# RetNet attention and a SwiGLU feed-forward block on one core: one explicit list for the order of all steps, in place of a list that ends early in the second up stage

## The chip, the cores and the metric

The kernel runs on one core of a Trainium2 chip. The metric is the device time of one execution in microseconds (us), median of several runs; lower is better. All other times here are from the hardware profile of one execution.

## What is computed

```python
def _attn_ref(q, k, v):                      # (4, 8, 768, 64) each
    for t in range(S):
        state = gamma * state + einsum('bhd,bhe->bhde', k[:, :, t], v[:, :, t])
        y[:, :, t] = scale * einsum('bhd,bhde->bhe', q[:, :, t], state)
    ...
x = attn_out.transpose(0, 2, 1, 3).reshape(3072, 512)
g = x @ w_gate                               # 512 x 1536
out = ((g * sigmoid(g)) * (x @ w_val)) @ w_out     # 1536 x 512
```

The three weights are float64 in the input; the rest is float32.

## The kernel before

**Stages.** The 3,072 tokens are worked off in four segments of 768 tokens, numbered 0 to 3: three chunks of 128 positions of two batches each. Each segment has an *up* stage (gate and value products, SiLU, their product, over 12 blocks `f` of 128 hidden columns) and a *down* stage (the product with `w_out`, over the same 12 blocks, into six banks of PSUM, one for each 128 tokens). The attention of segment `s + 1` is computed inside the down stage of segment `s`. The attention of segment 0 and the conversion of the weights from float64 words stand at the start, beside the up stage of segment 0.

**Products.** Every large product is made as three matmuls of fp32r parts: each operand is split into three tiles, by a step on ScalarE (ACT), then one on VectorE (DVE), then one on GpSimd (POOL) or DVE. From segment 1 on an up block is seven products in the manner of Strassen. Each is six matmuls of 384 columns.

**Steps and their names.** The program is a set of named steps, and each step issues some instructions, mostly on one engine:

- `s/pF.N` (line 933): product N of up block F of segment s, on TensorE (PE). Products 0, 2, 4 and 6 add into one bank, 1 is alone in a bank, and 3 and 5 add into a third.
- `s/uF.N` (lines 954 to 961): the ten steps between these products. `u.0`, `u.3` and `u.4` are copies by ACT out of a bank (shown at lines 955, 956 and 957). `u.0` must be through before product 2 of its block, `u.3` before product 4, `u.4` before product 5; `u.5`, on DVE, before product 6. `u.2` and `u.8` are SiLUs on ACT.
- `s/wF.G.0`, `.1`, `.2` (lines 921 to 931): the split of weight group G of up block F, on ACT (line 846), DVE (line 849) and POOL (line 852). Group 0 is for products 0 to 2, group 1 for 3 to 5, group 2 for 6. `s/LF` (line 911) loads the block's weights.
- `s/DF.T` (line 1000): three matmuls of 512 columns, block F, 128 tokens number T, into bank T. `s/hF.0` to `.2` split the hidden tile of block F, `s/WF` (line 980) loads the split `w_out` rows of block F into a ring of three tiles. In segment 0 these rows are split there as well (`0/dF.0` to `.2`) and stored for later (`0/ZF`).
- `s/eT` (line 1007): the copy of bank T into slot `T % 4` of the tile `chunk_x`, and the store of 128 finished rows. Even T are copied by ACT (line 1023) and odd T by DVE (line 1021). T = 5 of the last segment is done in halves: one by ACT, which issues its own store (lines 1015 and 1016), and one by DVE with a store from SyncE's queue (SP; lines 1017 and 1018).
- Attention of the next segment, for pair of chunks P: `scP.G` scores, `decP.G.I` the decay mask, `mP` and `oP` mixing with the values and the old state, `tP` the new state, all fp32 matmuls at line 638 or the steps that follow them; `yP.K` copies the result out of PSUM on ACT (line 874), `sumP.M` and `xP.N.K` make the operand of the next up stage. `s/lN` loads the N-th of its inputs. Keys without a slash are the same kind of steps for the start and the weight conversion (`s0`, `m0`, `A0`, `A1`, `l1:0`, `G7:1`).

**What sets the order.** Engines work in the order in which instructions were issued to them, and so does SP, which issues nearly all DMAs and waits in that order. Waits between engines are added by the framework from the tiles that each step reads and writes. `down_stage`, `up` and `up3` enter each step with a due time that is worked out from tables (`at(t, key, ...)`). `run` then issues:

```python
for key in PLAN.split():
    if key in events:
        events.pop(key)[2]()
    else:
        do(key)
for key in sorted(events, key=lambda k: events[k][:2]):
    events[key][2]()
```

So the steps that `PLAN` names come first, in its order, and all others follow by their due times. `PLAN` names 825 of the 2,312 steps: the start, up and down stage of segment 0, and of the up stage of segment 1 the products up to `1/p3.4`. Its last words are `1/p3.4 0/e4`.

Of the kernel before, what the change touches and what calls it, by code (L numbers as in the profile page):

```python
# [46 lines left out]


PLAN = """
    l0:0 A1 A0 s0 l1:0 l0:2 U0:0 A2 s1 l0:3 l2:0 K0 a0:1 l2:1 m0 b0:1 S0:1 c0:1 x0:1 V0:0 l1:3  # L50
    k1 a0:0 x0:2 C0:1 b0:0 n0:0 l1:2 t0 l2:2 l3:1 s2 l2:3 l3:0 Q2 m1 U1:1 g2 S0:0 c0:0 l3:2 n0:1
    k2 t1 o2 l4:0 x1:1 x1:2 g3 m2 C0:0 s3 n0:3 l4:1 q3 t2 o3 a1:1 n0:2 p0:0 x2:2 n0:4 b1:1 S1:1
    l3:3 g4 a1:0 c1:1 x2:1 n0:5 m3 k3 s4 C1:1 v0:0 b1:0 x3:1 x3:2 u0:0 l5:0 l5:1 U2:0 S1:0 t3
    c1:0 n1:0 s5 n1:1 l5:2 g5 C1:0 y0:0 p0:1 T0:0 a2 n1:3 T0:1 n1:4 q4 v0:1 q5 u0:1 U12:3 l4:2
    n1:2 o5 n1:5 T1:0 m5 y0:1 p1:0 b2 u1:0 U3:1 a12 S2 o4 p1:1 m4 a3 x5:1 v1:0 T0:2 T1:1 v1:1
    u1:1 U4:0 x4:1 c2 x5:2 x4:2 p0:2 b12 C2 y1:1 p1:2 T1:2 b3 n2:0 v1:2 y1:0 u0:2 Z0 U5:1 S3
    v0:2 n2:1 c12 n2:2 G2:0 u1:2 c3 L3 n2:3 S12 y0:2 U13:2 C3 a4 y1:2 b4 G2:1 C12 Z1 n3:0 n2:4
    S4 T2:0 T2:1 n2:5 i2:1 n3:3 n3:1 Z12 T2:2 U6:0 i2:0 c13 U14:3 a13 W2:0 W2:1 j2:1 n3:4 n3:2
    Z2 j2:0 G3:1 b13 a5 c4 G3:0 S13 T3:0 C4 i3:0 n4:0 T3:1 n4:1 n4:3 T3:2 b5 U7:1 S5 a6 i3:1 c14
    n3:5 n4:4 W3:0 W3:1 j3:0 C13 j3:1 n4:2 T4:0 G4:0 c5 C5 n4:5 T4:1 G4:1 W4:1 i4:0 Z3 i4:1 Z13  # L60
    U8:0 T4:2 j4:1 W4:0 a7 n5:0 n5:1 b6 n5:3 S6 j4:0 a14 b14 n5:2 G5:0 n5:4 S14 Z4 n5:5 c6 i5:0
    a8 C14 T5:0 C6 G5:1 n6:0 b7 n6:1 i5:1 n6:2 n6:3 U9:1 T5:1 U15:2 Z14 W5:0 W5:1 S7 c7 G6:0
    n6:4 T5:2 U10:0 i6:0 Z5 a15 j5:0 C7 T6:0 G6:1 b8 n7:0 n6:5 n7:3 W6:0 i6:1 j5:1 T6:1 b15 T6:2
    l5:3 n7:1 l4:3 S8 Z6 c8 n7:4 n7:2 n7:5 T7:0 C8 a9 W6:1 k4 c15 j6:0 S15 T7:1 U11:1 b9 k5
    U16:3 j6:1 G7:1 C15 G7:0 n8:0 W7:0 i7:1 S9 i7:0 n8:3 t4 Z15 U17:2 n8:1 W7:1 j7:0 c9 C9 n8:2
    a10 n8:4 b10 t5 G8:0 j7:1 G8:1 n9:0 T7:2 i8:1 Z7 n9:3 n8:5 S10 c10 W8:0 T8:0 a16 n9:1 i8:0
    n9:4 b16 C10 n9:2 a11 n9:5 W8:1 j8:0 j8:1 P0 G9:1 S16 G9:0 T8:1 T9:0 n10:0 b11 T8:2 n10:3
    n10:1 L2 W9:1 i9:0 T9:1 i9:1 0/h0.0 S11 c16 T9:2 W9:0 n10:2 0/h0.1 G10:1 C16 Z8 c11 C11
    G10:0 n10:4 n10:5 n11:0 j9:1 Z16 W10:1 n11:3 P2 j9:0 0/h0.2 n11:4 P1 T11:0 i10:0 c17 n11:1
    T11:1 0/h1.0 L1 T11:2 n11:2 W10:0 i10:1 G11:1 j10:0 n11:5 G11:0 L0 0/W0 a17 T10:0 0/h1.1 b17  # L70
    Z11 0/W1 T10:1 0/d0.0 h0 S17 W11:0 T10:2 0/d0.1 j10:1 1/sc0.0 h1 i11:0 Z9 0/d1.0 i11:1 j11:0
    C17 0/d0.2 1/l3 W11:1 1/dec0.0.0 1/old0 0/d1.1 1/sc0.1 1/dec0.0.1 0/D0.0 0/h2.0 Z17 1/q0.1
    0/W2 j11:1 0/Z0 0/D0.1 0/D0.2 0/h3.0 1/dec0.1.1 1/dec0.1.0 1/k0.1 1/q0.0 0/D0.3 0/d2.0 1/m0
    1/k0.0 0/h1.2 0/h2.1 1/f0 0/D0.4 1/o0 1/y0.1 Z10 0/d1.2 0/D0.5 0/D1.2 1/y0.0 1/y0.4 0/h2.2
    0/D1.4 0/h3.1 1/l5 0/d2.1 1/y0.5 0/D1.1 0/d2.2 0/W3 1/y0.3 1/y0.2 0/D1.3 1/y0.6 1/t0 1/begin
    0/D1.0 0/h3.2 1/y0.7 0/D1.5 0/D2.0 1/sum0.0 0/Z1 1/sum0.1 1/sum0.2 1/new0 1/x0.2.0 1/l4
    0/D2.1 0/D2.4 0/d3.0 0/W4 0/h4.0 0/d3.1 1/sc1.0 0/h5.0 0/h4.1 0/d4.0 1/sum0.3 0/d4.1 0/D2.3
    0/Z2 0/D2.5 1/x0.1.0 0/d3.2 1/l7 0/h4.2 0/D2.2 1/x0.2.2 0/W5 1/dec1.0.1 1/dec1.0.0 1/x0.0.0
    0/D3.3 1/sc1.1 0/D3.0 1/x0.1.1 0/h6.0 0/D3.4 0/d4.2 0/Z3 0/D3.5 0/D3.1 0/D3.2 1/x0.0.1
    0/D4.2 1/dec1.1.0 1/q1.0 1/dec1.1.1 0/h5.1 0/D4.4 0/d5.0 1/k1.1 1/q1.1 0/D4.0 1/k1.0 1/l6  # L80
    0/W6 0/d6.0 0/h7.0 1/m1 1/x0.1.2 1/x0.2.1 0/D4.1 0/h5.2 0/D4.3 0/d5.1 1/x0.0.2 1/f1 1/o1
    1/old1 1/y1.4 0/d6.1 0/d5.2 1/y1.2 1/l8 0/Z4 1/y1.3 0/D4.5 1/l9 0/h6.1 0/d6.2 1/y1.0 1/y1.7
    0/D5.2 0/h6.2 0/h7.1 0/D5.0 0/D5.4 1/y1.1 1/y1.6 0/W7 0/d7.0 0/Z6 0/h8.0 0/h7.2 1/t1 1/new1
    0/D5.5 1/sum1.2 0/D5.1 0/D5.3 1/y1.5 1/sum1.0 0/h8.1 0/h9.0 0/Z5 1/sc2.0 0/D6.4 0/W8 0/D6.5
    0/d7.1 0/h8.2 1/dec2.0.1 0/D6.0 0/D6.1 1/dec2.0.0 0/d7.2 1/sc2.1 0/D6.2 0/d8.0 1/l10 0/D6.3
    1/sum1.1 0/h9.1 0/W9 0/d8.1 1/dec2.1.0 1/q2.0 1/x1.1.0 1/dec2.1.1 1/q2.1 0/D7.0 0/d8.2
    1/x1.2.0 0/h10.0 0/D7.3 0/h9.2 0/D7.4 0/D7.5 0/Z7 1/x1.2.2 0/D7.1 1/sum1.3 0/D7.2 0/Z8 1/m2
    0/D8.4 0/h11.0 1/x1.2.1 1/x1.1.2 0/h10.1 1/f2 0/D8.1 0/d9.0 1/x1.0.0 1/o2 1/l11 0/d9.1
    0/h10.2 0/D8.5 0/W10 1/y2.7 0/d9.2 0/D8.0 0/D8.2 0/D8.3 1/x1.1.1 0/D9.0 0/d10.0 1/y2.5
    0/h11.1 0/d10.1 1/L0 1/y2.4 1/y2.2 1/x1.0.2 0/h11.2 1/y2.6 0/D9.1 0/D9.4 0/D9.5 1/y2.1  # L90
    1/y2.3 0/d10.2 0/W11 0/D9.2 0/D10.4 1/x1.0.1 0/D10.0 0/Z9 0/d11.0 1/x2.2.0 1/x2.2.1 1/y2.0
    0/D10.2 1/L2 0/d11.1 1/w0.0.0 0/D10.1 1/x2.1.0 1/sum2.0 1/L1 0/D10.5 1/sum2.1 0/d11.2 0/D9.3
    1/sum2.3 1/sum2.2 0/Z10 0/D11.4 0/D11.2 1/x2.1.2 1/w0.0.1 1/w0.2.0 0/D11.5 1/w0.1.0 1/x2.0.0
    0/D10.3 1/x2.1.1 1/x2.0.1 0/D11.0 1/x2.0.2 1/w0.1.1 0/D11.1 1/w1.0.0 1/x2.2.2 1/w0.0.2
# [88 lines left out]
T0, UP0 = 30.0, 8.35  # L183
# [1010 lines left out]
```

## Time and profile before

| | |
|---|---|
| median of 3 runs | 663.07 us (662.98 to 663.95) |
| the profiled execution | 662.59 us, of which its span is 660.8 us |
| TensorE | 646.4 us busy, 98% of the span, granted clock 0.997 |
| VectorE, ScalarE, GpSimd | 474.2, 365.8 and 256.2 us busy |
| DMA | 140.57 MB, 213 GB/s over the span |
| up and attention 0, down 0 | 0 to 131.5, 131.5 to 201.7 us |
| up 1, down 1 | 201.7 to 294.0, 294.0 to 362.7 us |
| up 2, down 2 | 362.7 to 450.5, 450.5 to 517.8 us |
| up 3, down 3 | 517.8 to 606.8, 606.8 to 656.5 us |
| after the last matmul | 656.5 to 660.8 us |

Times in the views are from the start of the span. A row of the timeline has its start, its length, engine, line and operation, the tiles, and in brackets how long the engine was idle before it and what ended that. A matmul's end is modelled: in an unbroken row of matmuls each one's end lies 0.16 us behind the start of the next, so an idle time in a bracket is 0.16 us shorter than what PE lost.

### The profile page before, as it was taken

How to read it: one execution, taken by the hardware profiler on the slowest of the kernel's cores; microseconds unless marked ns; L12 is line 12 of the kernel's file. 1: busy time of each engine (PE TensorE's matmuls, PEld its weight loads, DVE VectorE, ACT ScalarE, POOL GpSimd, SP SyncE). 2: the span in 40 equal slices, each digit the busy share in tenths (PEclk: the TensorE clock that was granted, in tenths of full speed). 3: DMA queues.
4: the chain of work that ended last, by engine and by line, in shares of the span. 5: the costliest groups of instructions: out<-in, count | busy, mean ns of one | idle time of the engine just before them, and what ended most of it. 6: DMA issues, size and time to landing. Idle time of an engine off the chain costs nothing.

```text
span 660.8 us, 12868 instructions
## 1 busy us (share of the span) xinstructions
PE 646.4 (98%) x5000; PEld 584.6 (88%) x5000; DVE 474.2 (72%) x723; ACT 365.8 (55%) x735; POOL 256.2 (39%) x171
## 2 busy tenths in 40 slices
PE   6999999999999989999999999999999999999997
PEld 6899999977778989997778999998777999999885
DVE  4887888889888856676678676677776776668441
ACT  3777977586355645646536655655744555554111
POOL 0625553634226746630113656660100656652000
PEclk8999999999999999999999999999999999999999
DMA  9979996698695353455674544355767453332554
GB/s 329 351 259 365 369 358 223 224 342 302 232 324 198 125 197 132 156 199 192 214 264 165 204 134 144 118 187 191 245 219 251 141 193 125 112 103 98 191 191 143
DMA packets 50621, 140.57 MB, mean 213 GB/s; under 512 B 4992, under 2 KB 18048, under 8 KB 50560
## 3 DMA queue, kind: packets, MB, share of 16 engines
q1 hardware_dynamic: 50128, 139.10, 61.1%
q8 instruction: 39, 0.64, 0.4%
q10 hardware_dynamic: 432, 0.66, 0.3%
q14 instruction: 22, 0.18, 0.1%
HBM read 109.85 MB, written 29.88 MB: 211 GB/s over the span
## 4 chain that ended last, share of the span: by engine, by line
PE 61%; DMA 1%; ACT 1%; DVE 0%; issue 0%; SPq 0%; ACTq 0%; DVEq 0%
PE bank L940 35%; PE bank L1003 22%; PE bank L638 4%; DMA oitem<-wdnt 1%; ACT chunk_x L874 0%; DVE gitem L281 0%; SPq L632 0%; DVE gitem L849 0%; ACT xb L855 0%; ACT gitem L846 0%; ACT states L750 0%; DVE hT L957 0%; DVE hT L958 0%; DVE chunk_x L1017 0%; ACT tmp L955 0%
## 5 line engine op out<-in xcount | busy, mean ns | idle before, releaser
L1003 PE MATMUL bank<-oitem,gitem 128*128 128x512 f32 x864 | 212.4, 399 | 0.7 <-DMA oitem<-wdnt 0.5
L1003 PEld LDWEIGHTS bank<-oitem,gitem 128*128 128x128 f32 x864 | 158.9, 188 | 40.7 <-issue 2.8
L852 POOL TENSOR_TENSOR gitem<-gitem 128x768 fp32r<-128x768 f32 x72 | 137.5, 1927 | 106.5 <-DVE gitem L849 93.1
L940 PE MATMUL bank<-xa,gitem 128*128 128x384 f32 x864 | 156.8, 335 | 2.7 <-ACT tmp L955 2.5
L940 PEld LDWEIGHTS bank<-xa,gitem 128*128 128x128 f32 x864 | 150.4, 188 | 3.3 <-ACT tmp L955 2.8
L852 POOL TENSOR_TENSOR oitem<-oitem 128x256 fp32r<-128x256 f32 (+1 forms) x60 | 62.1, 1036 | 78.3 <-DVE oitem L849 73.5
L775 PE MATMUL bank<-x,oitem 128*128 128x384 f32 x480 | 84.4, 337 | 0.0
L775 PEld LDWEIGHTS bank<-x,oitem 128*128 128x128 f32 x480 | 82.9, 188 | 0.5 <-POOL oitem L852 0.3
L940 PE MATMUL bank<-xb,gitem 128*128 128x384 f32 x432 | 82.0, 336 | 0.9 <-ACT chunk_x L1023 0.9
L846 ACT ACTIVATE gitem<-loads 128x768 fp32r<-128x768 f32 x72 | 57.9, 841 | 39.4 <-issue 27.0
L940 PEld LDWEIGHTS bank<-xb,gitem 128*128 128x128 f32 x432 | 76.0, 188 | 1.7 <-ACT chunk_x L1023 1.2
L849 DVE SCALAR_TENSOR_TENSOR gitem<-gitem,loads 128x768 fp32r<-128x768 f32 x72 | 67.9, 980 | 1.1 <-ACT gitem L846 1.1
L846 ACT ACTIVATE gitem<-hT 128x768 fp32r<-128x768 f32 x48 | 40.0, 840 | 42.2 <-PE bank L1003 28.7
L849 DVE SCALAR_TENSOR_TENSOR gitem<-gitem,hT 128x768 fp32r<-128x768 f32 x48 | 46.0, 961 | 18.5 <-ACT gitem L846 18.5
L714 POOL TENSOR_TENSOR loads<-loads,tab 128x512 f32<-128x512 f32 x8 | 12.9, 1613 | 96.7 <-PE bank L638 96.7
L281 DVE SCALAR_TENSOR_TENSOR gitem<-gitem 128x768 fp32r<-128x768 f32 x48 | 47.3, 988 | 0.8
L874 ACT COPY chunk_x<-bank 64x256 f32<-64x256 f32 x72 | 25.5, 367 | 34.4 <-PE bank L638 33.6
L940 PE MATMUL bank<-xb,oitem 128*128 128x384 f32 x216 | 43.7, 338 | 0.0
L956 ACT COPY tmp<-bank 128x384 f32<-128x384 f32 x36 | 17.2, 478 | 46.6 <-PE bank L940 43.3
L959 DVE TENSOR_TENSOR hT<-hT,bank 128x384 f32<-128x384 f32 x36 | 19.9, 553 | 29.0 <-ACT bank L959 29.0
L957 DVE TENSOR_TENSOR hT<-bank,tmp 128x384 f32<-128x384 f32 x36 | 20.1, 558 | 26.8 <-PE bank L940 26.6
L940 PEld LDWEIGHTS bank<-xb,oitem 128*128 128x128 f32 x216 | 38.1, 188 | 0.0
(104 smaller groups left out, 775.4 us busy)
## 6 DMA issues: line engine op xcount, KB each, us to landing
loads<-wup SPq DMA_DIRECT2D x36, 896.0 KB, 4.8
oitem<-wdnt SPq DMA_DIRECT2D x36, 768.0 KB, 4.4
wdnt<-oitem SPq DMA_DIRECT2D x12, 768.0 KB, 4.8
wup<-first SPq DMA_DIRECT2D x9, 896.0 KB, 7.5
rawp<-in_w_gate_dram SPq DMA_DIRECT2D x12, 512.0 KB, 6.8
rawp<-in_w_val_dram SPq DMA_DIRECT2D x12, 512.0 KB, 6.6
rawp<-in_w_out_dram SPq DMA_DIRECT2D x12, 512.0 KB, 7.3
out_dram<-chunk_x SPq DMA_DIRECT2D x23, 256.0 KB, 2.1
```

The source lines that it names most:

```text
L281: stt(o, x, 1.0, y, op0=mul, op1=op)
L638: nc.tensor.matmul(o, a, b, start=start, stop=True, skip_group_check=True)
L775: nc.tensor.matmul(o, w[:, a, ts(b, P)], X0[:, a, i, NC - 1 - b], start=a == b == 0, stop=a == 2 and b == NC - 1, skip_group_check=True)
L846: act(o[0], x, AF.Copy, scale=CUT / FAR)
L849: stt(o[1], f32(o[0]), -FAR, x, op0=mul, op1=add)
L852: op(o[2], f32(o[0]), f32(o[1]), op=add)
L874: copy(cx[half[i], ds(2 * h, 2), c], y_both(h, i, c))
L940: nc.tensor.matmul(o, w[:, a, k], x[:, a, KH - 1 - k], start=start and a == k == 0, stop=a == 2 and k == KH - 1, skip_group_check=True)
L956: lambda: act(gate, c11, AF.Silu, scale=ONE), lambda: copy(u2, x),
L957: lambda: copy(p5, wb), lambda: tt(h1, x, p5, op=add),
L959: lambda: act(x, x, AF.Silu, scale=ONE), lambda: tt(h1, h1, x, op=mul))
L1003: nc.tensor.matmul(banks[tok], hs[f][:, a, ds(i * TH + u * P, P)], wo[f][:, a], start=f == a == 0, stop=f == NF - 1 and a == 2, skip_group ...
```

## The change

`PLAN` is replaced as a whole, and nothing else. The new list names all 2,312 steps, so no step is left to its due time. The steps themselves, their instructions and their tiles are the same; the order differs from the first steps on. The parts that the text below speaks of (before, then after):

```diff
-    l0:0 A1 A0 s0 l1:0 l0:2 U0:0 A2 s1 l0:3 l2:0 K0 a0:1 l2:1 m0 b0:1 S0:1 c0:1 x0:1 V0:0 l1:3
...
-    1/k0.0 0/h1.2 0/h2.1 1/f0 0/D0.4 1/o0 1/y0.1 Z10 0/d1.2 0/D0.5 0/D1.2 1/y0.0 1/y0.4 0/h2.2
-    0/D1.4 0/h3.1 1/l5 0/d2.1 1/y0.5 0/D1.1 0/d2.2 0/W3 1/y0.3 1/y0.2 0/D1.3 1/y0.6 1/t0 1/begin
...
-    1/p3.3 1/u1.7 1/u3.1 1/w4.0.2 1/u3.3 1/u2.8 1/p3.4 0/e4
+    l0:0 A0 A1 l1:0 s0 l0:2 l2:1 s1 U0:0 l0:3 l2:0 m0 a0:1 A2 x0:1 b0:1 l1:3 x0:2 S0:1 l1:2 c0:1
...
+    0/d1.2 0/D0.4 0/D0.5 0/h2.1 0/D1.4 0/Z0 1/q0.0 1/m0 1/l4 0/h3.1 0/D1.0 1/f0 1/o0 0/h4.0
...
+    0/D1.3 0/h5.0 1/l6 1/sum0.1 0/D2.4 1/x0.2.2 1/sum0.3 1/t0 1/l5 0/W4 0/h5.1 0/d3.0 0/D2.2
+    1/x0.1.0 0/D2.3 0/Z2 0/d4.0 0/d3.1 1/new0 0/D2.1 0/h5.2 1/l7 0/d3.2 1/sc1.0 1/x0.1.2 0/D2.5
...
+    1/w4.2.1 1/p4.1 1/p4.3 1/p4.4 1/L7 1/u3.9 1/w6.2.0 1/u4.1 1/u4.4 1/p4.5 1/u4.5 1/w5.1.2
+    1/w6.1.0 1/u4.6 1/w6.0.0 1/w6.0.1 1/p5.0 1/u5.0 1/w4.2.2 1/p4.6 1/p5.2 1/u4.8 1/w6.0.2
...
+    3/D10.0 3/D9.1 3/D10.2 3/D11.4 3/D11.5 3/D11.2 3/D11.0 3/D10.1 3/D11.1 3/e1 3/D11.3 3/e0
+    3/e3 3/e2 3/e4 3/e5
```

Before, the products and the `D` steps from `1/p3.5` on come in the plain order of their numbers, and the last steps are `3/D11.0 3/D11.1 3/e0 3/D11.2 3/e1 3/D11.3 3/e2 3/D11.4 3/e3 3/D11.5 3/e4 3/e5`, each copy behind its own `D`. After, products of two blocks and `D` steps of up to three blocks stand mixed.

## The prediction

> **What bounds the kernel now.** First the page's busy times, then the windows by stage:
>
> ```profile
> PE 646.4 (98%) x5000; PEld 584.6 (88%) x5000; DVE 474.2 (72%) x723; ACT 365.8 (55%) x735; POOL 256.2 (39%) x171
> ```
>
> ```profile
> core 0: us, PE busy (x) PEld busy (x) DVE busy (x) ACT busy (x) POOL busy (x), PEclk, DMA share, GB/s
> ...
> 131.50:201.70 70.20, 69.64 (x761) 54.61 (x754) 62.46 (x88) 41.58 (x99) 24.53 (x16) 1.00 0.87 300
> 201.70:294.00 92.30, 88.72 (x506) 87.76 (x505) 65.23 (x103) 49.37 (x96) 53.45 (x35) 1.00 0.46 162
> ...
> 362.70:450.50 87.80, 87.80 (x506) 87.80 (x505) 59.88 (x97) 48.50 (x94) 51.05 (x34) 1.00 0.47 161
> ```
>
> TensorE sets the end. The change neither adds nor removes a matmul, so it can win only what PE waits, 14.4 us (660.8 - 646.4), of which 5.1 lie in the first 20 us, under the first loads, and 4.3 after the last matmul. Up 2 has no wait; up 1, with the same work, takes 92.3 instead of 87.8 us. There the old list ends. The timelines of PE, ACT and SP around that end:
>
> ```profile
> 203.78 1.32 PE L940 MATMUL bank<-xb,gitem 128*128 128x384 f32 x6 [0.91 <-ACT chunk_x L1023]
> ...
> 230.37 1.31 PE L940 MATMUL bank<-xa,gitem 128*128 128x384 f32 x6 [0.21 <-ACT tmp L957]
> ...
> 237.29 0.97 PE L940 MATMUL bank<-xa,gitem 128*128 128x384 f32 x4 [2.46 <-ACT tmp L955]
> ```
>
> ```profile
> 234.88 1.57 ACT L846 ACTIVATE gitem<-loads 128x768 fp32r<-128x768 f32 x2 [4.56 <-PE bank L940]
> 236.36 0.47 ACT L959 ACTIVATE bank<-bank 128x384 f32<-128x384 f32 x1
> 236.77 0.47 ACT L955 COPY tmp<-bank 128x384 f32<-128x384 f32 x1
> ```
>
> ```profile
> 229.56 0.33 SPq L1024 DMA_DIRECT2D out_dram<-chunk_x  x1
> 229.94 1.40 SPq L912 DMA_DIRECT2D loads<-wup  x3
> ```
>
> Read backwards: PE waits 2.46 us for a copy of 0.47 (`1/u4.0`). In ACT's queue the copy stands behind two splits (`1/w5.1.0`, `1/w5.0.0`), which wait for the load of block 5. SP issued this load only at 229.94, behind the list's last word, `0/e4`. By due time it would have been earlier.
>
> **What goes.** An idle time counts with the 0.16 us by which a modelled end runs over the next start. Up 1: 0.91 + 0.21 + 2.46 + 3 x 0.16 = 4.06. Down 1: `1/D5.0` waits 0.52 for its load, 0.68 lost:
>
> ```profile
> 322.53 0.96 PE L1003 MATMUL bank<-oitem,gitem 128*128 128x512 f32 x3 [0.52 <-DMA oitem<-wdnt]
> ```
>
> Smaller ones, from start-to-start times against the usual (1.04 a product, 0.70 a `D`), at `1/p0.3`, `2/m1`, `2/t2`, `3/p0.1` and `3/D0.1`: 0.12 + 0.19 + 0.28 + 0.17 + 0.40 = 1.16. In all **-5.9** from 201.7 us on. Ahead of that: 1.08 in down 0 (`1/sc2.0`, at 171 us) and four of 0.2 to 0.27, **-1.95**. The new order moves all these places; I let all go and enter below what stands in their stead.
>
> **What comes.**
>
> *Start.* `A0` goes ahead of `A1`, some chunk loads ahead of weight loads, and `K0` behind three more DVE steps. The first loads land in the order of issue, 0.7 us each: `l1:2`, for which PE waited (1.6 us, `m1`), comes 1.4 us earlier, and `t0` two to three us later, in the gap that was there. I take 0, bounds -1 and +1.
>
> *Down 0.* DVE is busy 62.5 of 70.2 us, so its order counts. (a) Ahead of `1/m0` DVE has nine steps behind the scores (four masks at 0.55, `d0.2` 1.58, `j11:0` 0.56, `d1.2` 1.60, `h2.1` 0.95, `q0.0` 0.90: 7.8, less 0.08 overlap each, 7.1), against some 7.0 of PE work: 0.4 lost with the hand-overs. (b) `1/l5` moves in SP's queue behind `1/l6`, which must wait for `1/o0`. From there: hand-over 0.25, three issues of `l6` 2.3 (as now), the first of `l5` 0.5 to 1.5, and the landing, median
>
> ```profile
> loads<-in_q_t_dram SPq DMA_DIRECT2D x18, 256.0 KB, 4.5
> ```
>
> 7.6 to 8.6; PE has nine `D` (6.3), `t0` (1.1) and a switch (0.2) until `1/sc1.0`, 7.6. So 0 to 1 lost, up to 4.5 if it lands as now (8.5); I take 0.8. (c) Ahead of `1/sc2.1` DVE has `new1`, two x steps, `d8.2`, `h9.2`, an x step and two masks: 7.1, less overlap 6.5, against 6.6 from `t1`: 0.6 lost with hand-overs. And 0.5 for what I can't see: **+2.3**, bounds 0.5 and 6.
>
> *Handovers in up 1 and up 2.* At six places two splits of 0.84 stand right ahead of `u.0`, and both must wait for a product: `w6.1.0 w6.0.0 u5.0` behind `1/p4.5`. PE has `p5.0` and `p4.6`, 2.08, until `p5.2`. The chain is 0.24 (end to ACT's start) + 0.84 + 0.84 + 0.48 - 2 x 0.09 (overlap on ACT) + 0.05 = 2.27. 6 x 0.19 = **+1.1**, bounds 0 and 2.
>
> *Shorter leads.* The mixed `D` order keeps tiles of the ring of three longer. From the last `D` of block F-3 to the first of F there are 8.3 us and more now; after, 6.0 to 10.2 in down 1, 7.4 to 11.1 in down 2 and 6.3 to 8.4 in down 3. Issue and landing took 4.1 to 8.8 in down 1 (two of twelve over 7), up to 7.3 in down 2 and 5.4 in down 3. So one or two may be late in down 1; with other unseen waits in 430 us of new order **+1.2**, bounds 0 and 5.
>
> *The end.* Now each copy follows its `D`, and the last ones are
>
> ```profile
> 656.59 0.60 ACT L1023 ACTIVATE chunk_x<-bank 128x512 f32<-128x512 f32 x1 [1.55 <-PE bank L1003]
> 657.08 0.38 ACT L1015 ACTIVATE chunk_x<-bank 128x256 f32<-128x256 f32 x1
> 657.49 0.35 ACTq L1016 DMA_DIRECT2D out_dram<-chunk_x  x1
> 657.49 0.42 DVE L1017 TENSOR_SCALAR chunk_x<-bank 128x256 f32<-128x256 f32 x1 [1.66 <-ACT chunk_x L1015]
> 657.94 0.33 SPq L1018 DMA_DIRECT2D out_dram<-chunk_x  x1
> ```
>
> with the last issue 1.44 after the last matmul (656.5) and 2.86 from it to the end. After, `D11.4` and `D11.5` come first of the last block, but `e4` is still late. With T as the end of the last matmul: `D11.1` ends at T - 0.7, `e1` on DVE takes to T + 0.05, SP issues its store and then that of `e0` (at T + 0.46). `e4` writes the slot of `e0`, so it waits for this store to land (2.4 where a store follows another now, as in down 1): T + 2.85. Then `e4` 0.6, `e5`'s half on ACT, the half on DVE, its store at T + 4.25: 2.8 later than now, **+2.8**, bounds 2 and 3.5.
>
> **Sum:** 662.59 - 5.9 - 1.95 + 0 + 2.3 + 1.1 + 1.2 + 2.8 = 662.1 for the profiled execution. The median is 0.48 above it: **662.6**.
>
> The Trainium skill has a rule that speaks against a list with any long gap. The granted clock stays 1.00 in the window of up 1, with its 2.46 us gap. "TensorE: Matmul & The Clock Gate", Part 1, says that after an idle window of some 3.4 us PE falls to half its clock, and needs as long to come back; by that an unforeseen gap of this length would cost an estimated 1.7 us more, and no run here shows one.
>
> **Rivals.**
>
> *The list holds* (R1). For it: up 2 shows PE without a wait, so an order without waits exists, and the old list ran from 30 to 130 us almost without any. Then only handovers, 0.4 in down 0 and the end are paid: 662.59 - 7.85 + 1.1 + 0.4 + 2.8 = 659.0, median 659.5.
>
> *Late `w_out` tiles* (R2), slower than before. One mechanism, in down 1 to 3: `sW` steps are issued when the ring's tile comes free, in 6.0 to 7 us windows, behind input loads in SP's queue. It decides where a load needs more than its window: at 7.5 to 8.8, as two did now, each costs 1.5 to 2.5. Three of them, 6 us, in place of the 1.2: 667.4. Against it: most land in 4.2 to 4.5.
>
> *It doesn't do what it says* is excluded: all steps are in the list, none is left to due times.
>
> **Numbers.** My forecast's case (661 to 664.5) has 0.44, R1 0.28, R2 0.25, anything else 0.03. The range 659 to 667.5 takes in most of both. A measurement tells 0.2%, 1.3 us: faster (below 661.7) is R1 and the lower edge of the forecast, 0.37; within, 0.36; slower (above 664.4) R2 and the upper edge, 0.27. The likeliest case alone: 661 to 664.5.
>
> **What would show it.** Up 1 at 88 to 89 us without the gap at 237; six waits of about 0.03 on `L955` (0.19 less 0.16); waits at `1/sc1.0` for a load and at `1/sc2.1` for DVE; in the end `e4` idle until a store lands, and 7 us after the last matmul instead of 4.3. I am wrong if the end stays at 4.3, if down 0 loses over 5 us, or if down 1 to 3 show PE waiting for `oitem`.

## The result and the profile after

The median went from 663.35 us (five runs, 662.98 to 666.6) to **660.02 us** (five runs, 659.8 to 661.15): ratio 0.9945, 95% interval 0.992 to 0.997. The change makes the kernel 0.55% faster. The profiled execution of after took 660.02 us, with a span of 658.2 (line numbers of the new kernel are 126 higher: L940 is now L1066, L1003 is L1129, L955 is L1081, L849 is L975, L852 is L978, L1023 is L1149).

The page's busy times, the windows of down 0, of up 1 and of up 2, and the list of PE's waits (with how much, how often, the longest):

```profile
PE 646.4 (98%) x5000; PEld 584.8 (89%) x5000; DVE 492.6 (75%) x723; ACT 365.3 (55%) x735; POOL 258.6 (39%) x171
```

```profile
130.50:199.66 69.16, 68.63 (x741) 53.83 (x733) 59.83 (x88) 41.79 (x99) 24.81 (x16) 1.00 0.87 299
199.66:285.31 85.65, 85.63 (x487) 84.31 (x486) 68.10 (x96) 46.79 (x92) 55.47 (x35) 1.00 0.44 153
354.45:443.20 88.75, 88.74 (x502) 87.13 (x501) 65.68 (x97) 50.65 (x102) 53.56 (x35) 1.00 0.46 160
```

```profile
PE bank L635 <- DMA hT<-in_k_t_dram: 2.7, 2, 1.9
PE bank L1233 <- DVE warm L1248: 1.1, 1, 1.1
PE bank L1129 <- DVE oitem L988: 0.5, 1, 0.5
PE bank L691 <- DVE hT L656: 0.3, 1, 0.3
```

Up 1 no longer has a wait: 85.63 of 85.65 us busy, where before it was 88.72 of 92.30. (It has 487 matmuls there in place of 506, because three products come behind the first `D` step; at the 0.176 us a matmul of this window, 506 are 89.0 us.) Behind the start one wait is left, 0.5 us for `oitem`, in down 0. No load of `w_out` is in the list. What the list does not show are waits that a modelled matmul end covers; they are read from start to start: 0.16 to 0.17 us at `1/p5.2`, `1/p11.2`, `2/p3.2`, `2/p7.2` and `2/p9.2`, 0.18 at `1/p11.6`, and some 0.1 more at the next matmul behind each of them.

The end, on PE, ACT and SP:

```profile
647.82 3.19 PE L1129 MATMUL bank<-oitem,gitem 128*128 128x512 f32 x13
648.95 1.09 ACT L1149 ACTIVATE chunk_x<-bank 128x512 f32<-128x512 f32 x2 [13.78 <-PE bank L1129]
...
651.07 3.87 SPq L1150 DMA_DIRECT2D out_dram<-chunk_x  x5
653.98 0.60 ACT L1149 ACTIVATE chunk_x<-bank 128x512 f32<-128x512 f32 x1 [3.95 <-DMA out_dram<-chunk_x]
...
655.34 0.33 SPq L1144 DMA_DIRECT2D out_dram<-chunk_x  x1
```

The last matmul ends at 651.01; `e4` (653.98) has stood idle for 3.95 us until a store landed, and the kernel ends 7.2 us after the last matmul, where it was 4.3.

Where the time went, by the starts of stages in the two traces (us):

| | predicted | measured |
|---|---|---|
| start, to the first product of up 0 (21.87, now 20.84) | 0 | -1.03 |
| up 0 and down 0, to `1/p0.0` (179.80, now 178.82) | -1.95 + 2.3 = +0.35 | -0.98 |
| from `1/p0.0` to the last matmul (454.83, now 451.35) | -5.9 + 1.1 + 1.2 = -3.6 | -3.48 |
| after the last matmul (4.30, now 7.20) | +2.8 | +2.9 |
| the profiled execution | 662.1 | 660.02 |

### The profile page after: what moved, and what is told of

Its sections match the earlier page's. It is cut to its first block, busy times and chain, and to the rows that moved or that the text cites. A ratio compares the mean times of both kernels' runs of the same rounds, so it can differ in the third digit from the quotient of the medians.

```text
span 658.2 us, 12826 instructions
## 1 busy us (share of the span) xinstructions
PE 646.4 (98%) x5000; PEld 584.8 (89%) x5000; DVE 492.6 (75%) x723; ACT 365.3 (55%) x735; POOL 258.6 (39%) x171
## 4 chain that ended last, share of the span: by engine, by line
PE 96%; DVE 2%; DMA 1%; issue 0%; SPq 0%; ACT 0%; ACTq 0%; DVEq 0%
PE bank L1066 40%; PE bank L1129 31%; PE bank L901 13%; PE bank L764 6%; PE bank L919 3%; PE bank L720 1%; DMA hT<-in_k_t_dram 1%; PE bank L635 1%; PE bank L691 1%; PE bank L706 1%; DMA out_dram<-chunk_x 0%; DVE xa L407 0%; DVE oitem L988 0%; DVE loads L407 0%; DVE xa L988 0%
## 5 line engine op out<-in xcount | busy, mean ns | idle before, releaser
L1129 PE MATMUL bank<-oitem,gitem 128*128 128x512 f32 x864 | 213.3, 399 | 0.5 <-DVE oitem L988 0.5
L1129 PEld LDWEIGHTS bank<-oitem,gitem 128*128 128x128 f32 x864 | 158.9, 188 | 39.8 <-issue 2.9
L978 POOL TENSOR_TENSOR gitem<-gitem 128x768 fp32r<-128x768 f32 x72 | 138.5, 1928 | 106.6 <-DVE gitem L975 93.5
L1066 PE MATMUL bank<-xa,gitem 128*128 128x384 f32 x864 | 162.9, 337 | 0.0
L1066 PEld LDWEIGHTS bank<-xa,gitem 128*128 128x128 f32 x864 | 150.9, 188 | 2.6 <-ACT tmp L1081 1.8
L975 DVE SCALAR_TENSOR_TENSOR gitem<-gitem,loads 128x768 fp32r<-128x768 f32 x72 | 85.2, 1192 | 19.9 <-ACT gitem L972 14.3
L978 POOL TENSOR_TENSOR oitem<-oitem 128x256 fp32r<-128x256 f32 (+1 forms) x60 | 65.9, 1101 | 53.3 <-DVE oitem L975 43.8
L1066 PE MATMUL bank<-xb,gitem 128*128 128x384 f32 x432 | 85.2, 336 | 0.0
L1066 PEld LDWEIGHTS bank<-xb,gitem 128*128 128x128 f32 x432 | 76.0, 188 | 0.8 <-DVE hT L1085 0.2
L975 DVE SCALAR_TENSOR_TENSOR gitem<-gitem,hT 128x768 fp32r<-128x768 f32 x48 | 47.0, 990 | 21.0 <-ACT gitem L972 21.0
L1066 PE MATMUL bank<-xb,oitem 128*128 128x384 f32 x216 | 43.6, 337 | 0.0
L1066 PEld LDWEIGHTS bank<-xb,oitem 128*128 128x128 f32 x216 | 38.1, 188 | 0.4 <-DVE hT L1083 0.3
L975 DVE SCALAR_TENSOR_TENSOR oitem<-oitem,loads 128x256 fp32r<-128x256 f32 (+1 forms) x42 | 30.3, 724 | 2.3 <-ACT oitem L972 1.4
L984 POOL TENSOR_TENSOR oitem<-oitem 128x512 fp32r<-128x512 f32 x12 | 18.6, 1553 | 34.0 <-ACT oitem L981 32.6
```

The source lines that it names most:

```text
L975: stt(o[1], f32(o[0]), -FAR, x, op0=mul, op1=add)
L978: op(o[2], f32(o[0]), f32(o[1]), op=add)
L984: op(o[1], f32(o[0]), x, op=sub)
L1066: nc.tensor.matmul(o, w[:, a, k], x[:, a, KH - 1 - k], start=start and a == k == 0, stop=a == 2 and k == KH - 1, skip_group_check=True)
L1129: nc.tensor.matmul(banks[tok], hs[f][:, a, ds(i * TH + u * P, P)], wo[f][:, a], start=f == a == 0, stop=f == NF - 1 and a == 2, skip_group ...
```

## The experiments

Theory: the gain is a few waits that the old order made, above all the load held behind the store `0/e4`; the new list pays most of it back at its end. Rivals: the order of every later stage is what pays; or the start and down 0 do. All medians stand beside runs of the kernel before on the same chip (663.1 to 663.9); the chips differ from run to run, so two runs are compared by their ratios or by their traces. "PE" is the time from the first product of up 0 (`p0:0`) to the last matmul, which leaves out the start, "end" what follows it.

| run | median | ratio, 95% interval | PE | end |
|---|---|---|---|---|
| before | 663.35 | | 634.63 | 4.30 |
| after | 660.02 | 0.9945 (0.992 to 0.997) | 630.17 | 7.20 |
| old end | 657.57 | 0.9907 (0.9893 to 0.9921) | 631.44 | 3.46 |
| one word in the old list | 660.23 | 0.9947 (0.993 to 0.9964) | 630.86 | 4.30 |
| new list cut ahead of up 2 | 658.01 | 0.9927 (0.9904 to 0.995) | 631.87 | 4.32 |
| new list cut in up 1 | 657.1 | 0.9903 (0.9885 to 0.9921) | 630.05 | 4.32 |
| other slots for the last copies | 658.76 | 0.9935 (0.9914 to 0.9957) | 630.92 | 6.20 |
| two words in the old list | 659.55 | 0.9946 (0.9924 to 0.9969) | 630.36 | 4.31 |
| first part alone | 661.28 | 0.9968 (0.9947 to 0.9988) | 633.08 | 4.31 |
| second part alone | 663.62 | 1.0009 (0.9994 to 1.0025) | 631.48 | 7.19 |
| three repairs | 655.48 | 0.9888 (0.9869 to 0.9907) | 628.95 | 4.32 |
| two places changed | 655.51 | 0.9882 (0.9854 to 0.9911) | 627.98 | 4.31 |
| two other places | 656.28 | 0.9883 (0.9862 to 0.9905) | 629.33 | 4.30 |

Some expectations count the end of after as 6.56 us; the timeline has 7.2.

### The old end in the new list

```diff
-    3/D10.0 3/D9.1 3/D10.2 3/D11.4 3/D11.5 3/D11.2 3/D11.0 3/D10.1 3/D11.1 3/e1 3/D11.3 3/e0
-    3/e3 3/e2 3/e4 3/e5
+    3/D10.0 3/D9.1 3/D10.2 3/D10.1 3/D11.0 3/e0 3/D11.1 3/e1 3/D11.2 3/e2 3/D11.3 3/e3 3/D11.4
+    3/e4 3/D11.5 3/e5
```

> The new list with its last 13 steps in the old order: 3/D10.1, then each of 3/D11.0 to 3/D11.5 with its own copy and store right behind it. Theory (the end costs 2.3 us because the copy 3/e4 waits for the store of 3/e0): the time from the last matmul to the end falls from 6.6 to 4.3 us, no idle time ahead of 3/e4 for a store, the rest as in the changed kernel: 2.3 us less than it, about 657.7. Rival (the tail is bound by the bytes that are still to be stored, or PE's last steps get later by the same amount): 659 to 660.

657.57 us: 2.45 less than after. The end shrinks from 7.20 to 3.46 us, but a new wait comes, ahead of the last product. PE's wait, and the copy it waits for:

```profile
650.21 0.60 ACT L1149 ACTIVATE chunk_x<-bank 128x512 f32<-128x512 f32 x1 [0.85 <-PE bank L1129]
650.86 0.53 PEld L1129 LDWEIGHTS bank<-oitem,gitem 128*128 128x128 f32 x3 [1.17 <-ACT chunk_x L1149]
650.86 0.97 PE L1129 MATMUL bank<-oitem,gitem 128*128 128x512 f32 x3 [0.74 <-ACT chunk_x L1149]
```

Banks 4 and 5 are two halves of one tile, so `D11.5` waits for `e4` where `e4` stands ahead of it, 0.9 us. In the old list it does not: there each copy comes one `D` later (`3/D11.5 3/e4 3/e5`), so this end is the old one but for that shift, and the shift makes the wait. The end of the new list is a cost of the change, of 2 to 3 us.

### One word in the old list

```diff
-    1/p3.3 1/u1.7 1/u3.1 1/w4.0.2 1/u3.3 1/u2.8 1/p3.4 0/e4
+    1/p3.3 1/u1.7 1/u3.1 1/w4.0.2 1/u3.3 1/u2.8 1/p3.4 1/L5 0/e4
```

> The kernel before with one word more in its list: 1/L5 directly ahead of the last word 0/e4, so that the load of block 5 no longer stands behind this store in SP's queue. Theory (this one place made the 2.46 us gap): the gap at 1/p4.2 goes, the other gaps of up 1 stay (1.07 and 0.37): 2.6 us less than before, about 660.7. Rival (the end of the list leaves the queues in disorder, whatever comes last): the gap moves to a later product and the gain is under 1 us, 662.4 or more.

660.23 us, as much as the whole change brings. SP, ACT and PE of this run around the place:

```profile
219.73 0.81 SPq L1024 DMA_DIRECT2D out_dram<-chunk_x  x2
220.59 0.44 SPq L912 DMA_DIRECT2D loads<-wup  x1
230.42 0.33 SPq L1024 DMA_DIRECT2D out_dram<-chunk_x  x1
```

```profile
232.63 1.58 ACT L846 ACTIVATE gitem<-loads 128x768 fp32r<-128x768 f32 x2 [1.45 <-issue]
```

```profile
233.42 2.26 PE L940 MATMUL bank<-xb,gitem 128*128 128x384 f32 x12
235.53 4.32 PE L940 MATMUL bank<-xa,gitem 128*128 128x384 f32 x24
```

The load is issued at 220.59, right behind the stores of `e3` and `e2`, where it was at 229.94; the store of `e4` (230.42), which has to wait for its copy on ACT, no longer stands ahead of it. The two splits of block 5 start at 232.63 in place of 234.88, and PE goes on without the 2.46 us gap. The wait of `1/D5.0` for its load goes as well. So the load was the cause, and SP's order what held it; the old list's last word did the harm, not the due times that followed it. Not all of the gain is the word's: PE is 3.8 us shorter than before, of which 2.9 lie behind `1/p0.0`. The other 0.9 lie ahead of it, where the two lists are the same: the wait of `1/sc2.0` in down 0 that the trace of before has doesn't come in this run.

### The new list, cut short

The list of after ends ahead of `2/p0.0`, or ahead of `1/p3.5`; all later steps go by due time, the end included. The second cut, beside the list of after:

```diff
-    1/w4.1.1 1/p3.2 1/p3.5 1/u3.3 1/w4.0.2 1/u2.9 1/w3.2.2 1/p3.1
...
-    3/e3 3/e2 3/e4 3/e5
+    1/w4.1.1 1/p3.2
```

> The new list cut off ahead of 2/p0.0; the steps of up 2 to the end follow by their due times, as before the change. Theory (from up 2 on the due times were as good as the list, and the list costs handovers of 0.2 us and 2.3 us at the end): 2.3 to 3.2 us less than the changed kernel, 656.8 to 657.7. Rival (a list that ends leaves a gap, or the new order of up 2 to down 3 carries part of the gain): 659 to 661.

> The new list cut off ahead of 1/p3.5, as far as the old one went; all later steps by due time. In this list the loads 1/L5 and 1/L6 stand ahead of the cut and 0/e4 behind it. Theory (the old gap was the load behind the store, not the end of the list as such): no gap over 1 us in up 1, small ones of 0.2 to 0.9 in down 1 to down 3 as before the change, and the old end: 657.5 to 658.5. Rival (a list that ends in an up stage leaves the queues out of step): a gap of 2 to 3 us in up 1 again, 660 to 661.

658.01 and 657.1 us. The second has a list as long as the old one, and is 2.9 us faster than the list of all steps: the order of the stages behind it is not what pays, the due times do as well there, and they bring the old end with them (4.32 us). What is new in it against the old list is the part up to `1/p3.5`, where `L5` and `L6` stand ahead of the cut. The first missed its number by a wait at the cut, on PE and on DVE:

```profile
364.22 1.32 PE L980 MATMUL bank<-xb,oitem 128*128 128x384 f32 x6 [1.85 <-DVE hT L997]
```

```profile
363.01 0.69 DVE L1061 TENSOR_SCALAR chunk_x<-bank 128x512 f32<-128x512 f32 x1 [2.05 <-DMA out_dram<-chunk_x]
363.62 0.55 DVE L997 TENSOR_TENSOR hT<-bank,tmp 128x384 f32<-128x384 f32 x1
```

The copy of a bank waits for the store that still reads its slot of `chunk_x`, and the step that the product needs is queued behind the copy. So a list that stops can have its price where it stops, 2.0 us here and 2.6 in the kernel before, but at a good place it has little: 0.5 us at the products around the cut in up 1.

### Other slots for the last copies

```diff
-        t = chunk_x[:, ts(tok % 4, DM)]
+        t = tmp[:, ts(tok - 4, DM)] if s == NSEG - 1 and tok > 3 else chunk_x[:, ts(tok % 4, DM)]
```

> The new list, unchanged; only the copies of banks 4 and 5 of the last segment go into a tile that is free by then, in place of slots 0 and 1 of chunk_x. Theory (e4 waits for the store of e0 because it writes the slot that this store reads): the idle time of 3.95 us ahead of e4 on ACT goes; the kernel ends some 5.0 us after the last matmul in place of 6.56, 1.6 us less, 658.4 us beside 660.0. Rival (the end is set by the five stores themselves, one after the other in SP's queue and in the DMA engines): e4's copy moves but its store lands as late as now, and the time stays within 0.4 us of 660.0.

658.76 us; in the trace the end is 6.20 us where it was 7.20, 1.0 less and not 1.6. The copies on ACT, and then the GB/s of 40 equal slices of 12 us (0.3 us each), this run from 645, after from 646.5:

```profile
648.01 1.09 ACT L1149 ACTIVATE chunk_x<-bank 128x512 f32<-128x512 f32 x2 [13.78 <-PE bank L1129]
648.99 0.60 ACT L1149 ACTIVATE tmp<-bank 128x512 f32<-128x512 f32 x1
```

```profile
GB/s 0 0 0 0 0 0 0 0 0 0 0 0 0 0 0 0 0 0 0 249 365 403 369 396 369 389 403 362 396 376 382 358 338 89 0 0 0 0 0 0
```

```profile
GB/s 0 0 0 0 0 0 0 0 0 0 0 0 0 0 0 0 0 7 355 389 369 382 382 375 403 362 396 75 0 61 396 369 328 345 249 0 0 0 0 0
```

The theory was right in that the wait of 3.95 us goes: `e4` follows at once. But the transfers of after have a gap of some 0.8 us only, where they wait for `e4`; without it, 1.57 MB run in one piece at 340 to 400 GB/s for some 4.2 us, and the first of them starts 0.6 us behind the last matmul (650.08). So both causes stand one behind the other: the shared slot costs 1 us, and that all six copies come late, and their bytes with them, 1.9. In the old end the first three stores run beside matmuls.

### Two words in the old list

```diff
-    0/D11.3 1/p0.0 1/w1.2.0 0/e0 1/u0.0 0/Z11 0/e1 1/w0.1.2 1/p0.1 1/w1.1.0 1/w1.0.1 1/p0.2
+    0/D11.3 1/p0.0 0/e0 1/w1.2.0 1/u0.0 0/Z11 0/e1 1/w0.1.2 1/p0.1 1/w1.1.0 1/w1.0.1 1/p0.2
...
-    1/p3.3 1/u1.7 1/u3.1 1/w4.0.2 1/u3.3 1/u2.8 1/p3.4 0/e4
+    1/p3.3 1/u1.7 1/u3.1 1/w4.0.2 1/u3.3 1/u2.8 1/p3.4 1/L5 0/e4
```

> The list of before with two words placed anew: 1/L5 ahead of the last word 0/e4, as in the earlier run (660.2 us), and 0/e0 ahead of the split 1/w1.2.0 that waits for a store in ACT's queue. Theory: the wait of 1.07 to 1.5 us at 1/p0.1 goes, 658.9 us, ratio 0.993; the two words then do more than the new list as a whole. Rival (1/p0.1 waits for something else as well, such as its own weight split): under 0.4 us less, 659.9 us or more.

659.55 us; beside the run with one word the intervals lie on each other, so the medians settle nothing. In the trace `1/p0.1` no longer waits (1.34 us idle in the run with one word) and 0.2 is left at `1/p0.2`, but 0.75 is lost at `2/t2` (0.46 in the run with one word) and 0.71 at `2/D5.0` (nothing there), and of the 1.3 us 0.5 remain (630.36 after 630.86).

### Each part alone

First the new order up to `1/p0.0`, then the old words; second the old words up to `1/p0.0`, then the new order. The seam of the first (beside the new list) and of the second (beside the old one):

```diff
-    0/D11.5 1/w0.1.2 1/p0.0 1/p0.1 1/u0.0 1/x2.0.2 1/w1.1.0
+    0/D11.5 1/w0.1.2 1/x2.2.1 1/x2.0.2 1/p0.0 1/u0.0 0/e1 1/p0.1 1/w1.1.0
```

```diff
-    0/D11.3 1/p0.0 1/w1.2.0 0/e0 1/u0.0 0/Z11 0/e1 1/w0.1.2 1/p0.1
+    0/D11.3 1/w1.2.0 0/Z11 1/w1.0.1 0/e0 1/w1.0.2 0/e2 1/w0.1.2 1/p0.0 1/p0.1
```

> The one part alone: the order of the new list up to 1/p0.0 (start, up 0, down 0), from there the words of the old list in their old order, and the rest by due time; 1/L5 stays behind the store 0/e4. By the prediction's steps for this part (2.3 paid in down 0 for 1.95 won): +0.35, 663.6 us. By the two traces (from the start to the first product of up 1 1.4 us less, and 0/e0, which 1/p0.1 waited for, now stands ahead of the cut): 1.4 to 2.4 less, 660.9 to 661.9 us; up 1 keeps its wait of 2.6 us for the late load.

> The other part alone: the order of the old list up to 1/p0.0, from there the new list. By the prediction's steps (4.06 + 0.68 + 1.16 won, 1.1 + 1.2 + 2.8 paid): 0.8 less, 662.5 us. By the two traces (from the first product of up 1 to the last matmul 3.5 less, end 2.3 more): 1.2 less, 662.1 us; if the two parts add up, this run and the other part alone together make the 3.3 us by which the medians differ.

661.28 and 663.62 us: 1.8 less and 0.5 more than the kernel before of the same chip (663.09), together 1.3 less and not 3.3. The first is what its traces had promised, not what the prediction's steps give (663.6); both expectations of the second missed. Each has a wait at its seam: the first one that neither list has alone, the second the old list's wait at `1/p0.1` (1.08 us lost in before, 1.50 in the run with one word, 1.72 here), which the new list doesn't have. PE's waits there, of the first part and of the second part, and ACT in the second:

```profile
201.96 4.22 PE L941 MATMUL bank<-xa,gitem 128*128 128x384 f32 x19 [0.68 <-DVE xa L863]
```

```profile
202.86 1.31 PE L1065 MATMUL bank<-xb,gitem 128*128 128x384 f32 x6 [1.55 <-ACT chunk_x L1148]
```

```profile
201.90 0.42 ACT L971 ACTIVATE oitem<-loads 128x256 fp32r<-128x256 f32 x1 [2.44 <-DMA wdnt<-oitem]
202.22 1.07 ACT L1148 ACTIVATE chunk_x<-bank 128x512 f32<-128x512 f32 x2
```

In the first, `1/x2.0.2` on DVE takes 2.88 us in place of 1.22, beside GpSimd, and the products wait for it and for the copy behind it, 1.6 us from start to start. In the second, `0/e0` stands behind a split that waits for the store of a `w_out` block, as in the old list. So 1.6 us of the first part's gain are lost at its seam, and 1.7 of what the second lacks against the new list, 0.6 of them beyond what the old list loses there; what each part is worth by itself these runs can't say more closely. That the first part is faster by itself, in spite of its seam and of the 2.4 us wait for the late load that it keeps, speaks against a cost of 2.3 us in down 0.

### Repairs

The end of the run with the old end, but `3/e4` behind `3/D11.5`; the splits at the six handovers behind `u.0`; `0/d5.2` ahead of a longer step on DVE. Two of the eight places:

```diff
-    1/w6.1.0 1/u4.6 1/w6.0.0 1/w6.0.1 1/p5.0 1/u5.0 1/w4.2.2
+    1/w6.1.0 1/u4.6 1/p5.0 1/u5.0 1/w6.0.0 1/w6.0.1 1/w4.2.2
...
-    1/k1.1 0/D4.5 1/x0.0.2 1/m1 0/W7 0/d5.2
+    1/k1.1 0/D4.5 0/d5.2 1/x0.0.2 1/m1 0/W7
```

> The new list with three repairs. (1) The end in the order of before, except that 3/e4 comes behind 3/D11.5, so that the last product no longer waits for the copy of the other half of its tile. (2) At the six handovers the splits that stand ahead of u.0 on ACT come behind it. (3) 0/d5.2 ahead of 1/x0.0.2 on DVE. By the theory each product wait goes that its edit removes and nothing takes its place: against the run that had the end in the old order (657.6 us) 0.9 for the last product, 0.9 to 1.1 for the six handovers, 0.7 for 0/D5.4: 654.9 to 655.3 us, ratio to the kernel before 0.987. Rival (the waits are only passed on, since DVE and ACT have the same work in less time): the later splits are late for the next block, gaps of 0.2 to 0.5 come elsewhere, and the time stays above 656.5 us.

**655.48 us**, 4.5 less than after and 1.1% less than before. That is not the edits alone: four of its five executions, and not the profiled one, had a granted clock of 0.999, and after's five had 0.993 to 0.995; by PE and end of the two traces, which leave out the start, it is 4.1 us less. The handovers, the wait of `0/D5.4` and that of the last product are gone (628.95 us from `p0:0`, 2.5 less than with the old end alone), while the end grew from 3.46 to 4.32: the repair of the last product gave its 0.9 us back there. One wait was passed on, as the rival had it; PE and DVE:

```profile
244.83 1.31 PE L1066 MATMUL bank<-xb,gitem 128*128 128x384 f32 x6 [0.82 <-DVE hT L1085]
```

```profile
240.81 2.16 DVE L975 SCALAR_TENSOR_TENSOR gitem<-gitem,loads 128x768 fp32r<-128x768 f32 x1
```

The later split ends in a DVE step that takes 2.16 us in place of 0.95, and `1/p6.0` waits. Two further kernels changed this and one other place:

```diff
-    1/w6.1.0 1/u4.6 1/p5.0 1/u5.0 1/w6.0.0 1/w6.0.1 1/w4.2.2
+    1/w6.1.0 1/u4.6 1/w6.0.0 1/w6.0.1 1/p5.0 1/u5.0 1/w4.2.2
...
-    1/p0.2 1/u0.1 1/p1.0 1/x2.2.1 0/e1 1/p1.1
+    1/p0.2 1/u0.1 1/p1.0 0/e1 1/x2.2.1 1/p1.1
```

and, in the second kernel, `1/x2.2.1 1/u0.1 1/p1.0 0/e1` in place of the last line. In the first kernel `0/e1` writes a slot of `chunk_x` ahead of the step that reads it, so the operand of up 1 has other values there, and so has the output; its instructions are the same, and it stands here for their times alone.

> The kernel of the run with three repairs (655.5 us), with two places changed. 1/w6.0.0 and 1/w6.0.1 stand ahead of 1/u5.0 again, because their move had passed the handover's 0.17 us on as a wait of 0.98 us of 1/p6.0 for VectorE; and 0/e1 comes ahead of 1/x2.2.1 on DVE, since 1/p0.3 waited 0.45 us for it. Theory (each wait is worth what the trace shows): 0.98 + 0.45 less, 0.3 more, 654.4 us. Rival (the waits of VectorE behind GpSimd turn up wherever the order leaves least room, so one goes and another comes): 655.5 us as before, with a new wait of 0.5 to 1 us at another place.

> The kernel of the run with three repairs (655.5 us), again with two places changed. 1/w6.0.0 and 1/w6.0.1 stand ahead of 1/u5.0 as in the new list, as in the run after it. And 1/x2.2.1 comes ahead of 1/u0.1 on DVE, which is idle there for 1.27 us, so that 0/e1 and with it 1/p0.3 are earlier, and 0/e1 still follows the step that reads the tile it writes. Theory (each wait is worth what the trace shows, and the start's spread hides it in the medians): no wait over 0.2 us at 1/p0.3 and 1/p6.0, 627.7 to 628.2 us from p0:0 to the last matmul, where the run with three repairs had 628.95; median 654.4 to 655.0 us. Rival (1/x2.2.1 takes 2 us beside GpSimd, and 1/u0.1 and 1/p1.1 or 1/p0.3 wait for it): a new wait of 0.4 us or more there, and 628.4 or more from p0:0 to the last matmul.

655.51 and 656.28 us, beside 655.48, with nearly the same ratio. In the traces the first loses the two waits (627.98 us from `p0:0`, 1.0 less, as expected), and in the second the rival's wait comes: `1/x2.2.1` takes 2.08 us beside GpSimd, `1/u0.1` follows late, and `1/p1.1` loses 0.4. The medians no longer tell these three apart.

### The third split step on VectorE in up 1

```diff
-        at(t + c, f"{s}/w{f}.{g}.2", lambda: near_c(it["o"][0]))
+        at(t + c, f"{s}/w{f}.{g}.2", lambda: near_c(it["o"][0], both if s == 1 else pool))
```

> The new list; the third step of every weight split in up 1 is made on VectorE in place of GpSimd. Question: why does the second step of a split, 128x768 on DVE, take up to 2.6 us in the new order. Theory (a DVE step that reads and writes SBUF is slowed while GpSimd works beside it): in up 1, where GpSimd now does nothing, these steps take 0.95 us each, 27 to 29 us for all instructions of that line in place of 38.1, and in up 2 and up 3 they stay at 34 to 37. Rival (the moment in the order or the DMA traffic slows them): up 1 stays above 34 us for that line. The time itself rises, since DVE has some 25 us more to do in up 1; how much is not the question.

The time is 663.52 us in one run. The steps of line 975 on DVE in up 1, 2 and 3 (length of the window, busy time and their number):

```profile
198.63:289.05 90.42, 25.10 (x34) 1.00 0.42 149
357.94:446.74 88.80, 35.75 (x37) 1.00 0.46 159
514.89:608.34 93.45, 36.27 (x39) 1.00 0.37 128
```

In up 1, with GpSimd idle, these steps take 0.74 us in the mean, all shapes together; in up 2 and 3, with it, 0.97 and 0.93. In after the same line takes 37.7 us (35 steps) in up 1. The theory holds, the rival falls: the order only sets how often the two engines meet (27.8 us for 35 such steps in before's up 2, with GpSimd at work).

## Why the prediction was right in most of its parts and 2.6 us too high

The change of each step stands in the first table. Point by point:

- **What goes, from 201.7 us on, and the handovers: right.** The cause of the 2.46 us gap was read rightly, and one word in the old list confirms it. "By due time it would have been earlier" is right too, but for `L5` alone it needs no due time: it needs only to stand ahead of a store. Of the six handovers five came, at 0.16 to 0.17 us each in place of 0.19, and the sixth, at `1/p6.2`, at 0.09; as waits on `L1081` they don't show, since a modelled end covers them.
- **Shorter leads, +1.2: right in sum by luck, wrong in kind.** No product waits for `w_out` in any of the runs with the new order of down 1 to down 3, although two of these loads took 7.1 and 8.1 us in down 2, so rival R2 (667.4 us) never began. In its stead some 1.4 us come, from start to start: 0.5 at the next matmul behind the five handovers, 0.3 at `1/p11.6` and behind it, and places of 0.06 to 0.11 in up 1 to up 3. The switches from `D` steps to the attention's products cost what they did before.
- **The end, +2.8: right** (2.9), with `e4` idle for the store of its slot. The run with other slots shows that this was only the nearer of two causes: without it 1.9 of the 2.9 us would have stayed, for the bytes.
- **Down 0, +2.3: wrong, and this is the step that failed.** None of its three waits came: PE finds `1/m0`, `1/sc1.0` and `1/sc2.1` ready. Down 0 as a whole took 66.42 us after 66.84, and with the 1.08 that went this leaves 0.7 for all that is new. The 1.08 itself was a wait of this one trace: three other runs with the old order of down 0 don't have it and take 65.8 to 66.0 us, and five of the seven with the new order take 65.6. So the order gains 0.2 to 0.4 us there where the sum had a loss. DVE between the scores and `1/m0`, in after:

```profile
131.68 0.86 DVE L988 SCALAR_TENSOR_TENSOR oitem<-oitem 128x512 fp32r<-128x512 f32 x1
...
135.00 0.69 DVE L988 SCALAR_TENSOR_TENSOR oitem<-oitem 128x512 fp32r<-128x512 f32 x1 [0.42 <-POOL oitem L984]
135.61 0.95 DVE L975 SCALAR_TENSOR_TENSOR gitem<-gitem,hT 128x768 fp32r<-128x768 f32 x1
136.48 0.68 DVE L407 SCALAR_TENSOR_TENSOR loads<-loads,tab 128x512 f32<-128x512 f32 x1
```

  `0/d0.2`, `0/d1.2` and `1/q0.0` take 0.86, 0.69 and 0.68 us, where the sum had 1.58, 1.60 and 0.90 from the trace of before. The queue ends at 137.16, and PE is there at 138.23. The last mask ahead of `1/sc2.1` is likewise done 1.1 us early. Both sums took a step's duration as its own; it was that of a step beside GpSimd. The wait at `1/sc1.0` was missed for another reason: the three issues of `1/l6` took 1.7 us in place of 2.3, and the loads of `1/l5` landed 3.6 us behind their issue in place of 4.5, so they were there 1.7 us ahead of the product.
- **The wait that came instead** is 0.7 us at `0/D5.4`, for `0/d5.2`, which the prediction didn't name. Of seven runs with this order of down 0 two have it, this one and the one with the old end. PE, DVE and GpSimd in after, then DVE and GpSimd in the run with other slots, which does not have it:

```profile
163.26 1.19 PE L1129 MATMUL bank<-oitem,gitem 128*128 128x512 f32 x4 [0.53 <-DVE oitem L988]
161.43 1.77 DVE L988 SCALAR_TENSOR_TENSOR oitem<-oitem 128x512 fp32r<-128x512 f32 x1
160.73 1.92 POOL L984 TENSOR_TENSOR oitem<-oitem 128x512 fp32r<-128x512 f32 x1 [1.44 <-ACT oitem L981]
```

```profile
160.85 0.68 DVE L988 SCALAR_TENSOR_TENSOR oitem<-oitem 128x512 fp32r<-128x512 f32 x1
161.55 1.30 POOL L984 TENSOR_TENSOR oitem<-oitem 128x512 fp32r<-128x512 f32 x1 [2.85 <-DVE oitem L988]
```

  The same instruction takes 1.77 us where GpSimd started 0.7 us ahead of it, and 0.68 where GpSimd came after it.
- **The start, 0: too high.** It took 1.03 us less, at the edge of the bounds. With this start the first product of up 0 came at 19.16 to 22.63 us in ten runs, with the old one at 21.50 to 23.17 in four. Most of this spread goes with the granted clock of the first 24 us (the third number from the right). Four runs, in this order: other slots, after and three repairs, which have the new start, and two words in the old list, which has the old one:

```profile
0.00:24.00 24.00, 19.47 (x240) 17.13 (x241) 15.89 (x25) 11.79 (x26) 6.58 (x9) 1.00 0.98 341
0.00:24.00 24.00, 19.97 (x237) 17.89 (x237) 14.63 (x24) 11.50 (x24) 6.46 (x9) 0.93 0.98 338
0.00:24.00 24.00, 18.62 (x203) 16.66 (x204) 13.65 (x22) 9.99 (x20) 5.30 (x8) 0.86 0.94 326
0.00:24.00 24.00, 18.93 (x236) 16.83 (x236) 14.57 (x25) 12.66 (x30) 5.90 (x9) 0.93 0.97 343
```

  Their first products come at 19.16, 20.84, 22.63 and 21.50 us. At a clock of 0.93 six runs with the new start have 20.08 to 20.84 and three with the old one 21.50 to 21.87; at 0.86 three have 22.12 to 22.63 and one 23.17. So at the same clock the new start is some 1.2 us earlier in the mean, 0.7 at the least. PE's waits ahead of `p0:0` sum to 5.1 us in before and 4.0 in after: the one of 1.6 for the values is gone and the first for `hT<-in_k_t_dram` is 1.0 shorter, but one of 1.9 for a later load of that tile has come, so the loss that the sum set against the gain was too large.

With down 0 at 0.7 the sum is 660.5 us for the profiled execution; the 0.5 us to 660.02 are the start's 1.03 less what up 0 (0.56 won in place of 0.87) and the last two rows of the table fell short by. The result lies beside the number of case R1, "the list holds", 659.5 us, which had 0.28, and below the forecast's own case (661 to 664.5). In kind it is R1 in the handovers, in down 0 and at the end; R1 has no place for the 1.4 us behind the handovers and elsewhere, nor for the start's gain of 1.0, and that these two nearly cancel is luck. The forecast had R1's reading of down 0 but let an estimate of 2.3 us stand against it, from durations that it had not asked the reason of.

## What to carry to other kernels

Where a stage has a gap, look in the queue of the engine that issues the loads for what stands ahead of the late one; a single word placed anew was worth 2.9 us here from `1/p0.0` to the last matmul, the new order of all 2,312 steps 3.5, and its end gave 2.9 of these back. When an order is made anew, its last steps are priced apart: copies that bunch behind the last product bring their stores with them, and a slot they share adds a wait. And before a queue is summed from durations, each of them needs its shortest and its longest from the trace, and the reason for the difference. A wait that stands in one trace may belong to that execution and not to the order; other traces of the same order tell.

## What the runs showed of the hardware

A VectorE step with both inputs in SBUF is held up beside GpSimd: 0.68 and 1.77 us above, 1.22 (after) and 2.88 (first part alone) for `1/x2.0.2`, 0.41 (after) and 2.08 (second of the last two kernels) for `1/x2.2.1`. Two rows of after's up 1, DVE and then GpSimd:

```profile
238.76 2.15 DVE L975 SCALAR_TENSOR_TENSOR gitem<-gitem,loads 128x768 fp32r<-128x768 f32 x1
```

```profile
238.19 1.90 POOL L978 TENSOR_TENSOR gitem<-gitem 128x768 fp32r<-128x768 f32 x1 [2.12 <-DVE gitem L975]
```

GpSimd ends at 240.09, and the DVE step 0.82 later, about its own time (0.95): it waits, it is not slowed. The same holds in all of after: 124 such steps that no GpSimd step overlaps take 0.94 to 0.96 us, and the 25 that start while GpSimd works and lose 0.3 us or more take up to 2.60, but each ends 0.81 or 0.82 us behind the GpSimd step. Steps that take one input from PSUM stay at 0.54 to 0.56 us beside GpSimd. The Trainium skill, "SBUF — State Buffer", section "SBUF: two separate sides", says that the two engines share a port pair as a lock: whichever starts first holds it for its whole instruction, and the other is blocked; a DVE step with two SBUF inputs takes part in this where the GpSimd instruction reads SBUF, as here. These rows agree for the case that GpSimd starts first. In after DVE is 18.4 us longer busy than before (492.6 and 474.2) with the same instructions; PE lost nothing by it but the waits named above, and these come and go from run to run.

The start spreads by as much as the change is worth, 3.5 us between runs of one order, and goes with its granted clock (1.00, 0.93 or 0.86 over the first 24 us; from 24 to 640 us it is 1.00 in all traces). So medians of five executions don't tell half a us, and traces are compared from `p0:0` on.
